# Lanes of 512 and 256 columns in place of twice 384 in the first products of two expert layers

## The chip, the cores and the metric

The program runs on one core of a Trainium2 chip. The metric is the device time of one execution in microseconds, as the median of three runs. PE is the matrix engine (TensorE), DVE is VectorE, ACT is ScalarE, POOL is GpSimd, SP issues DMA transfers.

## The reference, cut to what matters

```
y[t] = scale * q[t] @ state,  state = gamma * state + outer(k[t], v[t])   # 2 batches, 8 heads, 768 steps, head size 64
x = y as 1536 tokens x 512
h = x @ w_in              # 512 -> 2048
x = silu(h) @ w_out       # 2048 -> 512
h = x @ w_in2
out = leaky_relu(h, 0.01) @ w_out2
```

A retention layer feeds two layers that each widen 1536 tokens from 512 to 2048 features, apply a function and narrow again. All is float32; a float32 product is made of three matmuls of rounded parts (high x high, high x low, low x high: `TERMS`).

## The kernel before, in words

The tokens are cut into 12 chunks of 128 and kept transposed: features on the partitions, tokens along the row. For the widening products they form two lanes of N = 768 / 2 = 384 columns on two halves: four column groups s = 0 to 3 of 384 tokens, lane p = s // 2, half s % 2. `xa` holds the even groups, `xb` and `b12` the odd ones, `tm` and `xf` (in the two `big` tiles) the unrounded sums, and `T4[p]` the rounded sums.

The widening takes 16 feature blocks in eight steps of two blocks a layer. A step is a two by two matrix product in seven products (Winograd's form): weights and tokens are added and subtracted first, then seven products make the four results. A product (`product`, L410 on) is six matmuls a lane, and `go` issues lane 0 and then lane 1: 12 matmuls. The order of a step is written out in `rest` (L1018 on): 6, 2, 5, 7, 1 of the next step, 4, 3. Products 1, 6, 7 and 4 accumulate in one PSUM pair X, so ScalarE copies X (`copy`) after 1, 6 and 7 before PE may add to it; VectorE adds results from the banks Z and V to the copies (`add`); ScalarE applies the function (`act`), and `keep` stores the step's result in HBM. The first two steps of layer 0 are `plain`: four results of 24 matmuls each, 12 a lane. The first two steps of layer 1 are issued by `lanes` (L991 on), lane by lane and interleaved, steps a and b, so that lane 0 can begin before lane 1's tokens are there; c is step 2.

The narrowing in layer 0 (`down`, L517 on) has 24 units: three sets of 512 tokens times eight feature blocks, 24 matmuls of 512 columns each. It fetches results with `fetch_g` and rounds them with `split_g`. After the last block of a set `finish_x` copies the sums out. The narrowing of layer 1 is class `Two`: one set of 512 tokens plain and four of 256 in seven products.

Weights come as packed words and are decoded: `words` (ScalarE, two calls; the second writes the tile `u`), `clamp`, `sign` or `signed`, `low` (VectorE). `split_a` and `split_s` round weights and their sums, `keep_s` makes four sums in `u` on VectorE and stores them, `keep_w` stores the words, `fetch_w` brings words back. The order on each engine is the order in which the program issues: tasks in lists (`up_tasks`, `lane_tasks`, `todo`) are called ahead of the product, or unit, with their number. Every engine works off its queue in order.

Of the kernel before, what the change touches and what calls it, by code (L numbers as in the profile page):

```python
# [18 lines left out]
C = 128  # L19
# [9 lines left out]
N = 384  # L29
ORDER = [b * NC + c for c in range(NC) for b in range(B)]  # L30
PER = N // C
# [13 lines left out]
def retention_moe_kernel(ctx: ExitStack, tc: tile.TileContext, att, w1, w2, cst, out):  # L45
# [55 lines left out]
    raw = [sb.tile([128, n, 2, 2, 512], F32, tag=t, name=f"att_{t}") for t, n in (("t1", 3), ("w5", 1), ("t0", 2))]  # L101
# [9 lines left out]
    def two(i, p):  # L111
        return big[i].rearrange("p (a h k n) -> p a h k n", a=2, h=2, k=2)[:, :, p]
# [223 lines left out]
    def place(p):  # L336
        t = free.pop(0)
        b12[p] = [t[:, n, :, 0:N] for n in range(2)]
        return t
# [37 lines left out]

    def store_x(j):
        s, c = divmod(j, PER)
        a, b = c * C, c * C + C  # L380
# [9 lines left out]
    def round_x(j, which=(0, 1)):  # L390
        s, c = divmod(j, PER)
        a, b = c * C, c * C + C
# [34 lines left out]
    class Step:  # L427
        def __init__(self, layer, i):
            self.layer, self.i, self.w = layer, i, (layer, 0, i)
            self.X = None  # L430
            if layer == 0 and i == 0:
                self.g = call.rearrange("p a b n -> p (a b n)").rearrange("p (f s n) -> p f s n", f=2, s=4)
            else:
                b = (i + layer) % 2
                self.g = big[b].rearrange("p (f s n) -> p f s n", f=2, s=4)

        def go(self, n):
# [7 lines left out]
            for p, o in enumerate(getattr(self, t)[0]):  # L445
                product(n, self.w, p, o[:, 0:N], n in (1, 2, 5), n in (2, 3, 4))


        def lane(self, n, p):
# [8 lines left out]
            product(n, self.w, p, o[:, 0:N], n in (1, 2, 5), n in (2, 3, 4))  # L458
# [11 lines left out]

        def block(self, f, half, c=slice(0, 2)):
            return self.g[:, f, half::2][:, c]

        def copy(self, n, x=None):
            for c, t in (x or self.X)[1]:
                nc.scalar.activation(out=ct[n][:, c, 0:N], in_=t[:, :, 0:N], func=AF.Copy)  # L476

        def add(self, f, half, n, t):
            for c, t in t[1]:
                nc.vector.tensor_tensor(  # L480
                    out=self.block(f, half, c), in0=t[:, :, 0:N], in1=ct[n][:, c, 0:N], op=ALU.add
                )

        def act(self, f, half, t=None):
            for c, i in [(slice(0, 2), None)] if t is None else t:
                o = self.block(f, half, c)
                i = o if i is None else i[:, :, 0:N]
# [5 lines left out]
        def keep(self):  # L493
            t = gscr[self.layer, self.i] = dram.tile([128, 2, 4 * N], F32, name=f"g{self.layer}_{self.i}")
            nc.sync.dma_start(out=t.rearrange("p f (s n) -> p f s n", s=4), in_=self.g)
# [8 lines left out]
    def fetch_g(layer, s, i):  # L504
# [4 lines left out]
        nc.sync.dma_start(out=t, in_=gscr[layer, i][:, :, s * T:s * T + T])  # L509
# [19 lines left out]
    def finish_x(s, ya, yb, whole=None):  # L529
        later = []  # L530
        at = s * T
        segments = []
        while at < s * T + T:
            e = min(s * T + T, (at // N + 1) * N)
            segments.append((at - s * T, e - s * T, at // N, at % N))
            at = e
# [14 lines left out]
    class Two:  # L551
# [12 lines left out]
        def load(n, t):  # L564
            s, i = divmod(n, Q)
            m = 256 if s else T
            at = 256 * s + 256 if s else 0
# [51 lines left out]
        def run(self):  # L619
            wt = [three(p) for p in range(2)]  # L620
            x = [sb.tile([128, 3, 4, 256], FR, tag=f"xa{p}", name=f"s{p}") for p in range(2)]
            x = [t[:, n] for t in x for n in range(3)]
            x += [sb.tile([128, 4, 256], FR, tag=f"xb{p}", name=f"s{2 + p}") for p in range(2)]
# [64 lines left out]
            def third(i):  # L688
                return split_2((1, 1, i), wt[(i - 2) // 3][:, (i - 2) % 3])
# [521 lines left out]
```

## Time and profile before

| what | us |
|---|---|
| median of three runs | 546.33 (546.29 to 546.64) |
| the profiled execution | 546.1 |
| its span, first to last instruction | 544.3 |
| TensorE busy | 537.7 |
| VectorE busy | 423.0 |
| ScalarE busy | 308.7 |

The stages as the timeline shows them: retention until 45.8 us, the two plain steps until about 81, the other steps of layer 0 until 167.5, its narrowing until 298.1, the steps of layer 1 until 415.4 and its narrowing until the end. A matmul's length in a row overlaps the next one's, so its price is read from the distance of two starts.

### The profile page before, as it was taken

To read this page: it belongs to the slowest core of one execution; us is meant where nothing else is said; L and a number is where in the kernel's file an instruction comes from. 1 tells how busy PE (TensorE), PEld (TensorE's weight loads), DVE (VectorE), ACT (ScalarE), POOL (GpSimd) and SP (SyncE) were. 2 spreads that over 40 slices of the span, in tenths; PEclk is the share of its full clock that TensorE was granted. 3 is DMA by queue.
4 is the path that set the end of the run, shared out by engine and by line. 5 is a ranking of instruction groups with operands and counts; after the bars stand their busy time and mean duration, and the time that the engine had idled before them with its cause. 6 is when DMAs were issued, how large, how long until landed. Compare 5 with 4: busy or idle time off the path is not lost.

```text
span 544.3 us, 8909 instructions
## 1 busy us (share of the span) xinstructions
PE 537.7 (99%) x3534; PEld 501.0 (92%) x3534; DVE 423.0 (78%) x576; ACT 308.7 (57%) x394; POOL 77.8 (14%) x72
## 2 busy tenths in 40 slices
PE   8999999999999999999999999999999999999996
PEld 6999999999998888888888999999999888999996
DVE  3999979999976885764888876777777478998893
ACT  2257857787766655544445676666556465544341
POOL 2880000344400000001500020322100000000000
PEclk9999999999999999999999999999999999999999
DMA  8992525788789959697284009887648986643521
GB/s 297 417 358 82 178 106 212 275 287 284 221 287 362 359 189 300 197 309 274 80 303 160 2 8 369 323 314 280 243 165 295 384 300 233 198 149 102 157 79 39
DMA packets 41818, 124.92 MB, mean 229 GB/s; under 512 B 3758, under 2 KB 12078, under 8 KB 39728
## 3 DMA queue, kind: packets, MB, share of 16 engines
q1 hardware_dynamic: 41456, 124.01, 64.4%
q8 instruction: 27, 0.44, 0.3%
q10 hardware_dynamic: 288, 0.34, 0.2%
q14 instruction: 15, 0.12, 0.1%
q0 software_dynamic: 32, 0.00, 0.0%
HBM read 83.44 MB, written 40.89 MB: 228 GB/s over the span
## 4 chain that ended last, share of the span: by engine, by line
PE 96%; DVE 2%; DMA 1%; issue 0%; ACT 0%; DVEq 0%; ACTq 0%
PE p L421 22%; PE b L421 16%; PE b L523 12%; PE p L523 12%; PE b L660 8%; PE p L660 6%; PE p L644 4%; PE b L644 4%; PE p L963 3%; PE b L963 3%; PE p L276 2%; PE b L293 2%; PE b L305 1%; DVE c L283 1%; DMA att_t<-att_dram 1%; PE b L319 1%
## 5 line engine op out<-in xcount | busy, mean ns | idle before, releaser
L421 PE MATMUL p<-tt,w 128*128 128x384 f32 x504 | 95.7, 336 | 0.0
L421 PEld LDWEIGHTS p<-tt,w 128*128 128x128 f32 x504 | 88.7, 188 | 0.1
L476 ACT ACTIVATE c<-p 128x768 f32<-128x768 f32 (+1 forms) x48 | 35.1, 731 | 44.9 <-PE p L421 33.7
L480 DVE TENSOR_TENSOR big<-b,c 128x384 f32<-128x384 f32 x84 | 43.6, 550 | 17.8 <-ACT c L476 10.8
L523 PE MATMUL b<-w,wt 128*128 128x512 f32 x216 | 54.8, 389 | 0.0
L523 PE MATMUL p<-w,wt 128*128 128x512 f32 x216 | 54.8, 389 | 0.0
L147 ACT ACTIVATE u<-ws 128x1024 int32<-128x1024 uint32 x32 | 36.4, 1137 | 29.5 <-DVE r L169 28.1
L205 DVE TENSOR_TENSOR w<-c,w 128x1024 fp32r<-128x1024 f32 x23 | 29.9, 1298 | 28.5 <-ACT w L203 28.5
L523 PEld LDWEIGHTS b<-w,wt 128*128 128x128 f32 x216 | 40.6, 188 | 8.4
L523 PEld LDWEIGHTS p<-w,wt 128*128 128x128 f32 x216 | 40.6, 188 | 8.4
L162 DVE SCALAR_TENSOR_TENSOR r<-ws,r 128x1024 int32<-128x1024 int32 x32 | 42.6, 1330 | 0.9
L169 DVE CUSTOM_DVE_ANT_0 r<-r,u 128x2048 uint16<-128x2048 uint16 x32 | 41.3, 1292 | 1.4
L199 POOL TENSOR_TENSOR sf<-r 128x256 f32<-128x256 f32 x18 | 16.8, 955 | 176.1 <-DVE r L169 71.7
L145 ACT ACTIVATE r<-ws 128x1024 f32<-128x1024 f32 x32 | 36.6, 1144 | 8.0 <-DMA ws<-w_dram 6.0
L203 ACT ACTIVATE w<-c 128x1024 fp32r<-128x1024 f32 x23 | 24.4, 1063 | 18.7 <-DMA c<-g 18.7
L421 PE MATMUL b<-tt,w 128*128 128x384 f32 x168 | 32.0, 336 | 0.0
L421 PE MATMUL b<-xb,w 128*128 128x384 f32 x168 | 31.9, 337 | 0.0
L421 PE MATMUL b<-xa,w 128*128 128x384 f32 x168 | 31.9, 337 | 0.0
L421 PE MATMUL p<-xa,w 128*128 128x384 f32 x168 | 31.9, 337 | 0.0
L205 DVE TENSOR_TENSOR w<-sf,w 128x1024 fp32r<-128x1024 f32 x15 | 18.3, 1223 | 15.2 <-ACT w L203 15.2
L421 PEld LDWEIGHTS b<-tt,w 128*128 128x128 f32 x168 | 29.7, 188 | 0.0
L421 PEld LDWEIGHTS p<-xa,w 128*128 128x128 f32 x168 | 29.5, 188 | 0.1
(168 smaller groups left out, 1080.4 us busy)
## 6 DMA issues: line engine op xcount, KB each, us to landing
ws<-w_dram SPq DMA_DIRECT2D x64, 512.0 KB, 5.4
g<-big SPq DMA_DIRECT2D x15, 1536.0 KB, 6.3
c<-g SPq DMA_DIRECT2D x30, 512.0 KB, 7.2
scr<-r SPq DMA_DIRECT2D x16, 512.0 KB, 5.7
r<-scr SPq DMA_DIRECT2D x16, 512.0 KB, 7.6
att_t<-att_dram SPq DMA_DIRECT2D x15, 512.0 KB, 9.4
c<-g SPq DMA_DIRECT2D x17, 256.0 KB, 3.6
r<-g SPq DMA_DIRECT2D x15, 256.0 KB, 3.5
```

Of the source, the lines that this page charges most:

```text
L145: nc.scalar.activation(out=r.bitcast(F32), in_=t[:, :, :, 1].bitcast(F32), func=AF.Abs)
L147: nc.scalar.activation(out=u, in_=t[:, :, :, 0].bitcast(U32), func=AF.Copy, scale=2.0 ** -29)
L162: nc.vector.scalar_tensor_tensor(out=r, in0=t[:, :, :, 1], scalar=-0x40000000, in1=r, op0=ALU.bitwise_and, op1=ALU.bitwise_or)
L169: nc.vector.tensor_tensor(out=r, in0=r, in1=u, op=ALU.add)
L205: nc.vector.tensor_tensor(out=l, in0=s, in1=h.bitcast(F32), op=ALU.subtract)
L421: nc.tensor.matmul(out=o, lhsT=a[:, ta, k * 128:k * 128 + 128], rhs=rhs(p, tb, k), start=(begin and m == 0), stop=(end and m == 5), skip_g ...
L476: nc.scalar.activation(out=ct[n][:, c, 0:N], in_=t[:, :, 0:N], func=AF.Copy)
L480: nc.vector.tensor_tensor(out=self.block(f, half, c), in0=t[:, :, 0:N], in1=ct[n][:, c, 0:N], op=ALU.add)
L523: nc.tensor.matmul(out=y, lhsT=l, rhs=r, start=(i == 0 and f == 0 and n == 0), stop=(i == Q - 1 and f == 1 and n == 2),)
L644: nc.tensor.matmul(out=y[m], lhsT=g[:, tg, c:c + 128], rhs=w[:, tw, 1 - f], start=(i == 0 and f == 0 and k == 0), stop=(i == Q - 1 and f = ...
L660: nc.tensor.matmul(out=y[at][:, 256 * half:256 * half + 256], lhsT=g[:, tg, b], rhs=w[:, tw, a] if sm is None else S[i][tw][:, sm], start= ...
L963: nc.tensor.matmul(out=y[m][0][p][:, 0:N], lhsT=a[:, ta, (A11, A21)[f] + kk // 2, k * 128:k * 128 + 128], rhs=x, start=(i == 0), stop=(i = ...
```

## The change

The lanes become unequal: lane 0 has 512 columns (tokens 0 to 511 on one half, 512 to 1023 on the other), lane 1 has 256 (1024 to 1279, 1280 to 1535). So lane 0 holds the first two sets of the narrowing and lane 1 the third. All tiles that were 384 wide a lane follow: `xa`, `xb`, `T4`, the weights' place `three` (four and two blocks instead of three and three), the result tiles `big` and their place in HBM, from which `fetch_g` now reads a third set in two pieces of 256 columns. Copies and `act` calls over both lanes run over 768 columns in one piece.

```diff
-N = 384
+LANE = (512, 256)
+AT = (0, 512)
+N = sum(LANE)
-PER = N // C
+START = (0, 512, 1024, 1280)
...
-                product(n, self.w, p, o[:, 0:N], n in (1, 2, 5), n in (2, 3, 4))
+                product(n, self.w, p, o[:, 0:LANE[p]], n in (1, 2, 5), n in (2, 3, 4))
...
+        g = gscr[layer, i].rearrange("p f (h n) -> p f h n", h=2)
+        if s < 2:
+            nc.sync.dma_start(out=t, in_=g[:, :, s, 0:T])
+        else:
+            nc.sync.dma_start(out=t.rearrange("p f (h n) -> p f h n", h=2), in_=g[:, :, :, T:N])
...
-            4: lambda: (load_next(), [round_x(j) for j in LATER[:5]]),
+            4: lambda: (load_next(), [round_x(j) for j in LATER[:4]]),
...
-                     (b, 6, 0), (b, 2, 0), (b, 5, 0), (b, 7, 0), (a, 1, 1), (b, 4, 0), (b, 3, 0),
+                     (b, 6, 0), (b, 5, 0), (b, 7, 0), (b, 2, 0), (b, 4, 0), (a, 1, 1), (b, 3, 0),
...
-                if (n, p) == (7, 1):
-                    s.act(0, 0)
...
                 s.lane(n, p)
+                if (n, p) == (7, 1):
+                    s.act(0, 0)
...
-            todo[21] += [lambda: split_s(n0), lambda: high_t(0, 0)]
-            todo[22] += [lambda: left_t(0, 0), lambda: high_t(0, 1)]
-            todo[23] += [lambda: left_t(0, 1), lambda: split_s(n1)]
+            todo[21] += [lambda: split_s(n0)]
+            todo[22] += [lambda: high_t(0, 0), lambda: left_t(0, 0)]
+            todo[23] += [lambda: split_s(n1), lambda: high_t(0, 1), lambda: left_t(0, 1)]
...
-                if n == 21:
+                if n == 22:
                     T4[0] = tt_tile(0)
...
-            at(15, lambda: left_t(1, 1))
-            for m, t in enumerate(up_tasks(1, 1)):
-                at((15, 17, 20, 22, 24, 26, 28, 28)[m], *t)
+            at(14, lambda: left_t(1, 1))
+            w2nd, n2, n3 = second_w[1][1], first_w[Q + 2], first_w[Q + 3]
+            at(9, lambda: words(w2nd, at=-1))
+            at(11, lambda: clamp(w2nd))
+            at(24, lambda: signed(w2nd))
...
+            at(26, lambda: low(w2nd))
+            at(28, lambda: keep_s(w2nd), lambda: keep_w(w2nd))
```

On PE a step of layer 0 stands as follows before; `p` and `b` are PSUM tiles (pairs and single banks), `xa`, `xb` and `tt` (= `T4`) hold tokens, `w` weights, and the numbers only tell buffers apart.

```order
L421 MATMUL p_916<-xa_64,w_669 128x384 x6
L421 MATMUL p_916<-xa_65,w_669 128x384 x6
L421 MATMUL b_989<-tt_667,w_670 128x384 x6
L421 MATMUL b_990<-tt_668,w_670 128x384 x6
```

And the same products now.

```order
L430 MATMUL p_915<-xa_64,w_668 128x512 x6
L430 MATMUL p_915<-xa_65,w_668 128x256 x6
L430 MATMUL b_988<-tt_666,w_669 128x512 x6
L430 MATMUL b_989<-tt_667,w_669 128x256 x6
```

The order of products and the number of matmuls stay; the first lane of each product is longer and the second shorter.

On DVE the end of `lanes` in layer 1, from the rounding of step 2's weights on, before: L480 is `add`, L205 the low half of a rounding, L151 and L155 `clamp`, L162 `sign`, L169 `low`, L183 the sums of `keep_s`, whose store follows them.

```order
L205 TENSOR_TENSOR w_86<-sf,w_86 128x1024
L480 TENSOR_TENSOR big_69<-b_2679,c 128x384 x2
L151 TENSOR_SCALAR r_75<-r_75 128x1024
L155 TENSOR_SCALAR r_75<-r_75 128x1024
L480 TENSOR_TENSOR big_68<-b_2728,c 128x384
L162 SCALAR_TENSOR_TENSOR r_75<-ws_72,r_75 128x1024
L480 TENSOR_TENSOR big_68<-b_2746,c 128x384
L169 ISA r_75<-r_75,u 128x2048
L183 TENSOR_TENSOR u<-r_75 128x256 x2
L183 TENSOR_TENSOR u<-u,r_75 128x256
L183 TENSOR_TENSOR u<-r_75,u 128x256
L480 TENSOR_TENSOR big_68<-b_2746,c 128x384
```

Now (L496 is `add`, L211 the low half, L168 `sign`, L175 `low`, L189 the sums):

```order
L496 TENSOR_TENSOR big_69<-b_2668,c 128x256 x2
L496 TENSOR_TENSOR big_68<-b_2713,c 128x256
L168 SCALAR_TENSOR_TENSOR r_73<-ws_72,r_73 128x1024
L211 TENSOR_TENSOR w_85<-sf,w_85 128x1024
L496 TENSOR_TENSOR big_68<-b_2729,c 128x256
L175 ISA r_73<-r_73,u 128x2048
L189 TENSOR_TENSOR u<-r_73 128x256 x2
L189 TENSOR_TENSOR u<-u,r_73 128x256
L189 TENSOR_TENSOR u<-r_73,u 128x256
L496 TENSOR_TENSOR big_68<-b_2729,c 128x256
```

`clamp` has moved ahead (it now stands among lane 0's work), and the low half of `split_s` has moved behind `sign`; the sums still follow the addition of (b, 2) in lane 1.

On ACT, the copy of product 7 of lane 1 and the function of the result before it, step a, before (L476 and L492 are `copy`, L491 and L507 `act`, L203 and L209 the high half of a rounding):

```order
L476 ACTIVATE c<-p_2525 128x384
L203 ACTIVATE w_86<-sf 128x1024
L491 ACTIVATE big_69<-big_69 128x2x384
L476 ACTIVATE c<-p_2525 128x384
L476 ACTIVATE c<-p_2572 128x384
```

Now:

```order
L209 ACTIVATE w_84<-r_75 128x768
L492 ACTIVATE c<-p_2512 128x256
L507 ACTIVATE big_69<-big_69 128x768
L492 ACTIVATE c<-p_2559 128x256
```

The copy stands ahead of the function, and the high half of `split_s` has moved behind.

## Rows read from the trace of the kernel before

**Rows 1.** The page: engine's busy time, share, instructions; share of the chain that ended last.

```profile
PE 537.7 (99%) x3534; PEld 501.0 (92%) x3534; DVE 423.0 (78%) x576; ACT 308.7 (57%) x394; POOL 77.8 (14%) x72
...
PE 96%; DVE 2%; DMA 1%; issue 0%; ACT 0%; DVEq 0%; ACTq 0%
```

**Rows 2.** Timeline of PE, a step of layer 0: start, length (us), line, operands, count.

```profile
102.52 2.24 PE L421 MATMUL p<-tt,w 128*128 128x384 f32 x12
104.60 2.25 PE L421 MATMUL p<-xa,w 128*128 128x384 f32 x12
106.69 2.27 PE L421 MATMUL p<-tt,w 128*128 128x384 f32 x12
...
115.09 2.27 PE L421 MATMUL b<-tt,w 128*128 128x384 f32 x12
117.20 2.24 PE L421 MATMUL p<-tt,w 128*128 128x384 f32 x12
```

**Rows 3.** Timeline of PE, first row of the down stage and first row behind it.

```profile
167.49 1.52 PE L523 MATMUL b<-w,w 128*128 128x512 f32 x6
...
298.06 1.21 PE L421 MATMUL p<-xa,w 128*128 128x384 f32 x6
```

**Rows 4.** Timeline of PE, last stage, the same place in units 28 apart.

```profile
464.73 0.87 PE L660 MATMUL p<-wt,w 128*128 128x256 f32 x6
...
534.28 0.86 PE L660 MATMUL p<-wt,gh 128*128 128x256 f32 x6
```

**Rows 5.** Timeline of PE, 512 columns with weights from different places (second operand).

```profile
421.00 1.52 PE L644 MATMUL p<-w,w 128*128 128x512 f32 x6
422.36 1.52 PE L644 MATMUL b<-w,w 128*128 128x512 f32 x6
...
426.45 1.56 PE L644 MATMUL p<-wt,gh 128*128 128x512 f32 x6
427.85 1.56 PE L644 MATMUL b<-wt,gh 128*128 128x512 f32 x6
```

**Rows 6.** Groups by line and form, DVE: count, busy us, mean ns, idle before.

```profile
L480 DVE TENSOR_TENSOR big<-b,c 128x384 f32<-128x384 f32 x84 | 43.6, 550 | 17.8 <-ACT c L476 10.8 <-PE b L421 6.1 <-DMA g<-big 0.7
...
L372 DVE TENSOR_TENSOR tt<-big,tt 128x1536 fp32r<-128x1536 f32 x8 | 13.9, 1753 | 3.3 <-ACT tt L368 3.3
...
L677 DVE TENSOR_TENSOR o<-b,o 128x512 f32<-128x512 f32 x8 | 5.5, 692 | 0.8
...
L677 DVE TENSOR_TENSOR o<-p,o 128x256 f32<-128x256 f32 x4 | 1.7, 418 | 4.4 <-ACT o L676 4.4
```

**Rows 7.** Timelines of DVE and of PE, layer 0: one addition three steps apart, and PE.

```profile
98.98 1.01 DVE L480 TENSOR_TENSOR big<-b,c 128x384 f32<-128x384 f32 x2
...
143.21 1.01 DVE L480 TENSOR_TENSOR big<-b,c 128x384 f32<-128x384 f32 x2
...
144.45 2.27 PE L421 MATMUL b<-tt,w 128*128 128x384 f32 x12
```

**Rows 8.** Timeline of ACT, first copy of layer 1.

```profile
299.36 0.49 ACT L476 ACTIVATE c<-p 128x384 f32<-128x384 f32 x1 [1.12 <-PE p L421]
```

**Rows 9.** Timelines of PE, DVE, SP and ACT, end of `lanes` and step 2 of layer 1.

```profile
322.14 1.21 PE L421 MATMUL b<-xa,w 128*128 128x384 f32 x6
...
339.94 2.27 PE L421 MATMUL p<-tt,w 128*128 128x384 f32 x12
...
323.39 0.56 DVE L480 TENSOR_TENSOR big<-b,c 128x384 f32<-128x384 f32 x1 [0.20 <-PE b L421]
...
329.36 0.33 SPq L185 DMA_DIRECT2D scrs<-u  x1
...
336.75 1.18 ACT L147 ACTIVATE u<-ws 128x1024 int32<-128x1024 uint32 x1 [1.41 <-DMA scrs<-u]
...
338.56 0.80 ACT L476 ACTIVATE c<-p 128x768 f32<-128x768 f32 x1
```

**Rows 10.** Transfers of `scrs`, the stored sums: from issue to landing.

```profile
DMA to landing us min/median/max: 2.6/3.9/10.0
```

More of the change, by code (lines that the diff above doesn't have):

```diff
@@ L337, in place @@
         t = free.pop(0)
-        b12[p] = [t[:, n, :, 0:N] for n in range(2)]
+        b12[p] = [t[:, n, :, 0:LANE[p]] for n in range(2)]
         return t
@@ L376, in split_t, with columns @@
         left_t(p, n)
+    def columns(j):
+        s = max(n for n in range(4) if START[n] <= j * C)
+        return s, j * C - START[s], j * C - START[s] + C
     def store_x(j):
-        s, c = divmod(j, PER)
-        a, b = c * C, c * C + C
+        s, a, b = columns(j)
         y = yu[j]
@@ L469, in lane, with cols @@
                 self.add(0, 1, 1, t(o))
+        @staticmethod
+        def cols(c, t=None):
+            if t is None:
+                return slice(AT[c.start], AT[c.stop - 1] + LANE[c.stop - 1])
+            return t.rearrange("p a n -> p (a n)")[:, 0:sum(LANE[c])]
         def block(self, f, half, c=slice(0, 2)):
-            return self.g[:, f, half::2][:, c]
+            return self.g[:, f, half, self.cols(c)]
         def copy(self, n, x=None):
             for c, t in (x or self.X)[1]:
-                nc.scalar.activation(out=ct[n][:, c, 0:N], in_=t[:, :, 0:N], func=AF.Copy)
+                nc.scalar.activation(out=flat[n][:, self.cols(c)], in_=self.cols(c, t), func=AF.Copy)
         def add(self, f, half, n, t):
@@ L480, in add @@
                 nc.vector.tensor_tensor(
-                    out=self.block(f, half, c), in0=t[:, :, 0:N], in1=ct[n][:, c, 0:N], op=ALU.add
+                    out=self.block(f, half, c), in0=self.cols(c, t), in1=flat[n][:, self.cols(c)], op=ALU.add
                 )
@@ L493, in keep @@
         def keep(self):
-            t = gscr[self.layer, self.i] = dram.tile([128, 2, 4 * N], F32, name=f"g{self.layer}_{self.i}")
-            nc.sync.dma_start(out=t.rearrange("p f (s n) -> p f s n", s=4), in_=self.g)
+            t = gscr[self.layer, self.i] = dram.tile([128, 2, 2 * N], F32, name=f"g{self.layer}_{self.i}")
+            nc.sync.dma_start(out=t.rearrange("p f (h n) -> p f h n", h=2), in_=self.g)
         def done(self):
@@ L530, in finish_x @@
         later = []
[L531 to L536, printed above, removed]
+        segments = [(START[n] - s * T, START[n] - s * T + LANE[n // 2], n, 0) for n in range(4) if START[n] // T == s]
         for k, y in ((1, yb), (0, ya)):
@@ L566, in load @@
             m = 256 if s else T
-            at = 256 * s + 256 if s else 0
+            at = (0, N, N + 256, T, N + T)[s]
             nc.sync.dma_start(
@@ L620, in run @@
             wt = [three(p) for p in range(2)]
-            x = [sb.tile([128, 3, 4, 256], FR, tag=f"xa{p}", name=f"s{p}") for p in range(2)]
-            x = [t[:, n] for t in x for n in range(3)]
-            x += [sb.tile([128, 4, 256], FR, tag=f"xb{p}", name=f"s{2 + p}") for p in range(2)]
+            x = [sb.tile([128, n, 4, 256], FR, tag=t, name=f"s{t}") for t, n in (("xa0", 4), ("xa1", 2), ("xb0", 2))]
+            x = [t[:, n] for t in x for n in range(t.shape[1])]
             S = [x[2 * n:2 * n + 2] for n in range(4)]
@@ L818, in retention_moe_kernel @@
             0: load_next, 2: lambda: (words(wa), clamp(wa)), 3: lambda: (signed(wa), low_a()),
-            4: lambda: (load_next(), [round_x(j) for j in LATER[:5]]),
-            5: lambda: ([round_x(j) for j in LATER[5:]], words(wb), clamp(wb), signed(wb)),
+            4: lambda: (load_next(), [round_x(j) for j in LATER[:4]]),
+            5: lambda: ([round_x(j) for j in LATER[4:]], words(wb), clamp(wb), signed(wb)),
         }
```

39 lines of the change are left out of this document (22 added, 17 removed).

## The prediction

> **What bounds the kernel now.** I read the page first: TensorE is busy for 537.7 of the 544.3 us and the chain that ended last is 96% PE [rows 1]. Then TensorE's timeline: from 45.8 us on no row shows idle time, so each product starts when the one ahead lets it. Two things can therefore move the end: the distance from one matmul's start to the next, and a wait that does not exist today.
>
> The distances come from starts, since a matmul's own length overlaps the next one. A step is seven products of 12 matmuls. From 102.52 to 117.20 us the 84 matmuls of 384 columns take 14.68 us, 174.8 ns each [rows 2]. The same rows show that the price depends on what came before: a product that reads `tt` after one that also read `tt` takes 2.08 us (173.3 ns a matmul), `xa` or `xb` after `tt` 2.09, and `tt` after `xa` or `xb` 2.11. Seven times 2.08 would be 14.56, so these changes of operand cost 0.12 us a step. The down stage has 576 matmuls of 512 columns from 167.49 to 298.06 us: 226.7 ns each [rows 3]. The last stage has 588 matmuls of 256 columns between 464.73 and 534.28 us (28 units of 21): 118.3 ns each [rows 4].
>
> **The shapes.** Number of matmuls and sum of columns stay; each pair 384 + 384 becomes 512 + 256. A step becomes 42 x 226.7 + 42 x 118.3 = 9.52 + 4.97 = 14.49 us, 0.19 less. There are six such steps in layer 0 and eight in layer 1 (two of them in `lanes`, by lane, in the same number): 14 x 0.19 = 2.7 us. The two `plain` steps have 96 matmuls of 384 each, 16.78 us at 174.8 ns, and will have 48 x 345.0 ns = 16.56: 0.22 each, 0.4 together. That is 3.1 us, the upper bound of the gain. It supposes that the changes of operand go, as the rows of the down stage show none. But that stage doesn't alternate between operands and the new steps still do. The lower bound from the same rows: 173.3 ns at 384 and 226.7 at 512 lie on a line of 0.417 ns a column plus 13.3 ns; on it 256 columns cost 120.0, a step 42 x 346.7 ns = 14.56, and with the 0.12 kept it is 14.68 again: gain nought. I take the measured 118.3, which also comes from a stage that alternates, and half of the changes: 3.1 - 14 x 0.06 - 0.1 = **2.2 us** gained.
>
> One row goes further down. In the last stage's first unit 512 columns take 1.36 us per six when weights come from `w`, but 1.40 when they come from a `gh` that lies in the place of `ws` [rows 5]: 233.3 ns instead of 226.7. There it is the stationary operand; in lane 0 `xa` and `xb` are the moving one, and at 384 columns they cost no more than `tt`. I leave it out of the sum and keep it as the third rival.
>
> **Vector and scalar work.** Copies and `act` calls over both lanes keep their 768 elements. An addition of 384 took 550 ns, twice 1.10; 512 and 256 take 692 and 418, together 1.11 [rows 6]. The copies of `finish_x` become fewer. All of it lies beside PE. What counts is where PE arrives sooner than its partners.
>
> First, layer 0. VectorE's additions for one product of successive steps start at 98.98 and 143.21 us, three steps apart: 14.74 us a step, PE 14.68 [rows 7]. At 143.21 lane 0's addition ends 0.55 us later, and PE writes that bank at 144.45: 0.69 us left. The addition of 512 ends 0.14 later, and with a PE step of about 14.55 four steps lose another 4 x 0.13 = 0.52. So 0.03 remain: **0**; with the full shape gain (4 x 0.19) it would be a wait of some 0.2, bounds 0 to 0.3.
>
> Second, lane 1 in `lanes`. A product of a lane shrinks from 1.04 to 0.71 us. Between the end of (a,7) and the start of (a,4) lies one product, and the copy of 7 must be through. Such a copy began at 299.36, 0.26 us after its product was issued in full (298.06 + 6 x 0.173), and takes 0.49 at 384 elements and 0.80 at 768, so 0.39 at 256 [rows 3, 8, 9]: 0.65 of 0.71. The change puts this copy ahead of `act(0, 0)`, which keeps it so. Price 0 to 0.1, taken 0.05.
>
> Third, step 2 of layer 1. Its product 4 waits for the copy of product 7, which stands on ScalarE behind the second half of `words`; that half writes `u` and waits until the store of `u` issued by `keep_s` has landed. Before: product (b,2) of lane 1 starts at 322.14 and product 4 at 339.94, 17.80 later. The addition behind (b,2) starts at 323.39, the store is issued 5.97 later, `u` is free 7.3 after that (336.75 less the start-up), and the copy ends at 339.36, 0.58 before PE needs it [rows 9]. After: 3 x 0.71 + 2.07 + 2 x 0.71 + 5 x 2.07 = 15.97 us from (b,2) to product 4. The addition starts at 0.71 + 0.21 = 0.92. Behind it VectorE has, start to start, the addition itself (0.34), `sign` (1.14), the low half of `split_s` (1.14), an addition (0.34), `low` (1.25) and the four sums (1.55): 5.8. With the same 7.3 for the store and 2.7 to the end of the copy that is 16.7: PE waits **0.7 us**. The moved `clamp` and `words` stand earlier and hide behind lane 0. The bounds lie in the store: the transfers of this kind landed between 2.6 and 10.0 us after issue [rows 10], this one with the 1.5 MB store of `g` just ahead of it on the same queue. A landing within 6.6 us removes the wait, one of 10 makes it 3.4. I take 7.3, the row at this very place.
>
> `T4[0]` is now made after unit 21 instead of 20, so its first half is rounded in unit 22. Unit 21 ends at 167.49 + 22 x 5.44 = 287.2 (24 units in 130.57 us), and (a,5) reads the half 12 us later. VectorE's share of a rounding takes 1.75 us at 1536 elements [rows 6], some 2.3 at 2048, ScalarE's comes ahead of it; the splits of `n0` and `n1` and the four sums that stand between fill the rest only in part. Cost nought; if that cover went, (a,5) waits for what is left over.
>
> **Sum.** 546.1 (the profiled execution, 544.3 of span and 1.8 around it) - 2.2 + 0.7 + 0.05 + 0 = 544.65. The median of the three runs is 0.23 above this execution, so 544.9 on the median.
>
> **Rivals.** (1) Full shape gain and the store lands sooner: -3.1 with 0.2 to 0.9 of waits, 543.4 to 544.1. For it: six matmuls of 512 columns from like places take the same 1.36 us in each row [rows 5]. Against: every us PE gains makes the waits above longer. (2) No gain in the shapes: cost is linear in columns and the changes of operand stay, so 0 to -0.5 with 0.7 of waits: 546.3 to 547. For it: the line through 384 and 512. The Trainium skill, in "TensorE: Matmul & The Clock Gate", section "Back-to-back issue gap", gives a warm gap of N / 2.4 plus a fixed 2.5 ns; by it both splits of 768 columns cost 325 ns and the shapes bring nothing. The trace has 13.3 where the page has 2.5, but agrees that 384 and 512 lie on a line; 118.3 at 256 lies below it. (3) Slower: 512 columns with operands from unlike places cost 233.3 [rows 5]. If all 684 matmuls of lane 0 do, that is +4.5 against -3.1, with 0.8 of waits +2.2: 548.5. It decides from 231.2 ns (349.5 - 118.3) on, where a pair costs the old 349.5. If only the 324 that read `xa` or `xb` do, it is +2.1, and the end stays within 0.2 of today.
>
> **How the numbers follow.** Forecast 0.40, own range 544.1 to 545.7; rival 1 0.17; rival 2 (with the milder form of 3) 0.29; rival 3 0.14. A measurement of this kernel can tell about 0.2%, 1.1 us, from no change: faster means below 545.2, slower above 547.4. Faster: 0.17 and 0.24 of the forecast = 0.41. Within: 0.16 of the forecast and 0.26 of rival 2 = 0.42. Slower: 0.14 and 0.03 = 0.17. Range 543.9 to 547.7: it leaves out the best of rival 1 and the worst of rival 3.
>
> **What would show it.** In the trace after: a step of layer 0 in 14.5 to 14.6 us (shapes right), 14.68 or more (rival 2 or 3), with six lane-0 matmuls at 1.36 against 1.40 telling rival 3; a PE gap of some 0.7 us before product 4 of step 2 of layer 1, released by the copy, with `u` waiting for the store just ahead on ScalarE; no gap at the change of layers above 0.1. The prediction is wrong if PE idles anywhere else, or if the pair 512 + 256 costs more than 349.5 ns.

## The result

The changed kernel takes 551.42 us (549.69 to 551.63, six runs) where the kernel before takes 546.22: a ratio of 1.009, interval 1.0077 to 1.0103. The forecast was 544.9 with a range of 543.9 to 547.7, so it was wrong in sign and size. The profiled execution of after took 551.4 us against 546.1, and its span 549.4 against 544.3. Its mean granted clock of 0.996 holds a fall that is shown below; two more of the six executions have 0.996 (spans of 549.1 and 549.6 us), and three have 0.999 (547.6 to 548.8), which leaves no room for such a fall.

The page says first that TensorE's busy time grew by only 2.5 us and that the chain that ended last, 96% PE before [rows 1], now runs through VectorE and ScalarE too. From the page of after, engines and chain:

```profile
PE 540.2 (98%) x3534; PEld 472.8 (86%) x3534; DVE 427.7 (78%) x573; ACT 307.9 (56%) x385; POOL 82.0 (15%) x72
...
PE 86%; DVE 7%; ACT 3%; DMA 2%; issue 2%; DVEq 0%; ACTq 0%; SPq 0%
```

TensorE's timeline of after, one row for the start of each stage (start us, length, engine, line, operands, count). Starts are what is read; where the window that was asked for ends inside a row, here and further down, its length and count cover only the part inside:

```profile
45.64 4.70 PE L977 MATMUL p<-xa,w 128*128 128x512 f32 x19
...
167.51 1.53 PE L543 MATMUL b<-w,w 128*128 128x512 f32 x6
...
298.08 1.56 PE L430 MATMUL p<-xa,w 128*128 128x512 f32 x6
...
420.47 1.56 PE L658 MATMUL p<-w,gh 128*128 128x512 f32 x6
```

| stage | before, us | after, us |
|---|---|---|
| steps of layer 0 (45.8 to 167.5) | 121.65 | 121.87 |
| narrowing of layer 0 | 130.57 | 130.57 |
| steps of layer 1 | 117.36 | 122.39 |
| narrowing of layer 1, to the end of the span | 128.9 | 128.9 |

Two things can be seen in it. Layer 0, which held some 1.1 us of the gain forecast, gained nothing: the shapes bring nothing there. And the whole loss of 5.03 us lies in the steps of layer 1.

A step of layer 0 after the change, which answers to [rows 2]:

```profile
102.48 2.26 PE L430 MATMUL p<-tt,w 128*128 128x512 f32 x12
104.58 2.28 PE L430 MATMUL p<-xa,w 128*128 128x512 f32 x12
106.69 2.24 PE L430 MATMUL p<-tt,w 128*128 128x512 f32 x12
108.77 2.28 PE L430 MATMUL b<-xb,w 128*128 128x512 f32 x12
...
117.16 1.09 PE L430 MATMUL p<-tt,w 128*128 128x512 f32 x4
```

The step is 117.16 - 102.48 = 14.68 us, to the hundredth what it was. The order of prices has turned round, though: before, `tt` behind `xa` was the dear one (2.11) and `xa` cost 2.09; now `xa` and `xb` cost 2.11 to 2.12, `tt` behind them 2.08, and `tt` behind `tt` 2.10 instead of 2.08.

The change of layers, timeline of PE (in brackets the idle time ahead and what ended it):

```profile
299.48 0.40 PE L430 MATMUL b<-tt,w 128*128 128x512 f32 x1
301.53 1.43 PE L430 MATMUL b<-tt,w 128*128 128x512 f32 x5 [1.65 <-DVE tt L378]
303.31 2.93 PE L430 MATMUL p<-tt,w 128*128 128x512 f32 x6 [0.35 <-ACT c L492]
306.03 1.73 PE L430 MATMUL b<-xa,w 128*128 128x512 f32 x6
```

and the stretch behind them by engine and granted clock (us, busy us and count for PE, PEld, DVE, ACT and POOL, PEclk, DMA share, GB/s):

```profile
303.31:306.44 3.13, 3.13 (x8) 2.51 (x8) 1.50 (x1) 1.15 (x4) 0.00 (x0) 0.51 0.00 0
```

The second product waits, one matmul in, for the low half of `T4[0]` (`left_t(0, 0)`, L378): 2.05 us from start to start instead of 0.23, and the next start comes 0.11 late. The third waits for the copy of the first (L492): another 0.52. Behind these two waits the granted clock is 0.51, the lower level of 1.2 GHz, over 3.13 us: seven matmuls, which take some 1.61 at full clock, lose 1.5. Before, the same stretch had a clock of 1.00 and no idle time.

At step 2 of layer 1, timelines of PE, ACT, SP, DVE and POOL:

```profile
342.03 2.27 PE L430 MATMUL p<-xa,w 128*128 128x512 f32 x12
344.85 1.43 PE L430 MATMUL p<-tt,w 128*128 128x512 f32 x5 [0.54 <-ACT c L492]
...
342.20 1.16 ACT L153 ACTIVATE u<-ws 128x1024 int32<-128x1024 uint32 x1 [1.60 <-DMA scrs<-u]
...
336.65 0.33 SPq L191 DMA_DIRECT2D scrs<-u  x1
...
328.93 0.42 DVE L496 TENSOR_TENSOR big<-b,c 128x256 f32<-128x256 f32 x1 [1.06 <-PE b L430]
331.87 1.65 DVE L175 CUSTOM_DVE_ANT_0 r<-r,u 128x2048 uint16<-128x2048 uint16 x1
333.55 1.73 DVE L189 TENSOR_TENSOR u<-r 128x256 f32<-128x256 f32 x2
...
331.70 2.42 POOL L205 TENSOR_TENSOR sf<-r 128x256 f32<-128x256 f32 x2 [58.31 <-DVE w L211]
```

This is the wait that the prediction named, in its place: product 4 starts 0.70 us after the one ahead of it would let it (342.03 + 2.12 = 344.15), with 0.1 more on the next matmul.

The account of the profiled execution: 1.82 + 0.11 + 0.52 of waits at the change, 1.5 of clock, 0.80 at step 2, 0.07 in lane 1: 4.8 of the 5.03 us. What is left, 0.2, is spread over dearer products, in the lanes and in the steps behind them.

### The profile page after: what moved, and what is told of

Its sections match the earlier page's. It is cut to its first block, busy times and chain, and to the rows that moved or that the text cites. A ratio compares the mean times of both kernels' runs of the same rounds, so it can differ in the third digit from the quotient of the medians.

```text
span 549.4 us, 8898 instructions
## 1 busy us (share of the span) xinstructions
PE 540.2 (98%) x3534; PEld 472.8 (86%) x3534; DVE 427.7 (78%) x573; ACT 307.9 (56%) x385; POOL 82.0 (15%) x72
## 4 chain that ended last, share of the span: by engine, by line
PE 86%; DVE 7%; ACT 3%; DMA 2%; issue 2%; DVEq 0%; ACTq 0%; SPq 0%
PE p L430 20%; PE b L430 15%; PE b L674 8%; PE b L543 8%; PE p L543 8%; PE p L674 6%; PE p L658 4%; PE b L658 4%; PE p L977 3%; PE b L977 3%; PE p L282 2%; DVE w L211 2%; PE b L299 2%; PE b L311 2%; PE b L325 1%
## 5 line engine op out<-in xcount | busy, mean ns | idle before, releaser
L430 PE MATMUL p<-tt,w 128*128 128x512 f32 (+1 forms) x504 | 97.1, 340 | 0.9 <-ACT c L492 0.9
L430 PEld LDWEIGHTS p<-tt,w 128*128 128x128 f32 x504 | 81.0, 191 | 12.3 <-ACT c L492 1.8
L492 ACT ACTIVATE c<-p 128x768 f32<-128x768 f32 (+2 forms) x48 | 35.0, 732 | 46.3 <-PE p L430 32.9
L496 DVE TENSOR_TENSOR big<-b,c 128x512 f32<-128x512 f32 (+1 forms) x84 | 43.5, 551 | 20.7 <-ACT c L492 10.4
L211 DVE TENSOR_TENSOR w<-c,w 128x1024 fp32r<-128x1024 f32 x23 | 29.5, 1282 | 28.2 <-ACT w L209 28.2
L168 DVE SCALAR_TENSOR_TENSOR r<-ws,r 128x1024 int32<-128x1024 int32 x32 | 44.4, 1387 | 0.9
L205 POOL TENSOR_TENSOR sf<-r 128x256 f32<-128x256 f32 x18 | 17.5, 991 | 175.7 <-DVE r L175 71.4
L175 DVE CUSTOM_DVE_ANT_0 r<-r,u 128x2048 uint16<-128x2048 uint16 x32 | 41.9, 1309 | 1.8 <-DVE r L168 0.5
L151 ACT ACTIVATE r<-ws 128x1024 f32<-128x1024 f32 x32 | 36.6, 1144 | 8.9 <-DMA ws<-w_dram 6.6
L209 ACT ACTIVATE w<-c 128x1024 fp32r<-128x1024 f32 x23 | 24.2, 1060 | 19.3 <-DMA c<-g 19.2
L430 PE MATMUL b<-tt,w 128*128 128x512 f32 (+1 forms) x168 | 32.0, 337 | 1.6 <-DVE tt L378 1.6
L430 PE MATMUL b<-xa,w 128*128 128x512 f32 (+1 forms) x168 | 32.4, 340 | 0.0
L430 PE MATMUL b<-xb,w 128*128 128x512 f32 (+1 forms) x168 | 32.2, 339 | 0.0
L430 PE MATMUL p<-xa,w 128*128 128x512 f32 (+1 forms) x168 | 32.2, 339 | 0.0
L430 PEld LDWEIGHTS b<-tt,w 128*128 128x128 f32 x168 | 26.7, 189 | 5.4 <-DVE tt L378 2.1
L430 PEld LDWEIGHTS b<-xa,w 128*128 128x128 f32 x168 | 27.2, 190 | 3.8
```

Source lines behind the costliest of these rows:

```text
L151: nc.scalar.activation(out=r.bitcast(F32), in_=t[:, :, :, 1].bitcast(F32), func=AF.Abs)
L168: nc.vector.scalar_tensor_tensor(out=r, in0=t[:, :, :, 1], scalar=-0x40000000, in1=r, op0=ALU.bitwise_and, op1=ALU.bitwise_or)
L175: nc.vector.tensor_tensor(out=r, in0=r, in1=u, op=ALU.add)
L211: nc.vector.tensor_tensor(out=l, in0=s, in1=h.bitcast(F32), op=ALU.subtract)
L430: nc.tensor.matmul(out=o, lhsT=a[:, ta, k * 128:k * 128 + 128], rhs=rhs(p, tb, k), start=(begin and m == 0), stop=(end and m == 5), skip_g ...
L492: nc.scalar.activation(out=flat[n][:, self.cols(c)], in_=self.cols(c, t), func=AF.Copy)
```

## Experiments

Theory after the result: (P) the operands' places, that is, where their tiles start in a partition of the on-chip memory, and the hand-over between column counts set what a product costs, so the shapes bring nothing; (G) the four operations on lane 0's sums that GpSimd does in unit 18 grew from 768 to 1024 elements, and VectorE, slowed beside them, delivers everything behind them late. Rivals: the waits come from the order in which `T4` and the splits are issued, from the redone order as a whole, or from the 512 columns themselves. Every kernel was timed against the kernel before on its chip.

### Shapes: places of the operands

e1_after_place and e2_before_place move three small tiles, which shifts the start of `xa` and `xb`, and of the tiles behind them (`ws`, and so `gh`, among them), from 224 bytes behind a multiple of 512 to the multiple itself, where `tt` and the weights lie. Below, two operands in like places both start at the multiple or both 224 bytes behind one; otherwise their places are unlike.

```diff
+    z = sb.tile([128, 256], BF, name="z")
+    z1 = sb.tile([128, 1], F32, name="z1")
+    one = sb.tile([1, 64], F32, name="one")
     xa = [sb.tile([128, 2, NP, LANE[p]], FR, tag=f"xa{p}", name=f"xa{p}") for p in range(2)]
```

> The changed kernel, with the three small tiles z, z1 and one made ahead of xa, so that xa, xb, big, c and ws begin at a multiple of 512 bytes in their partition, as the weights and tt do (before: 224 behind one). Nothing else moves. Theory P (the operand's place costs): six matmuls of 512 columns from xa or xb take 1.36 us instead of 1.39, a product 2.08, a step of layer 0 14.55 us instead of 14.68; 14 such steps give 1.8 us, and the last stage 0.8, since its 120 matmuls with a gh from a ws place fall from 233.3 to 226.7 ns. In all -2.8, 548.6 us. Theory H (the hand-over from 256 to 512 columns costs, whatever the place): tt after tt, both at multiples of 512, costs 2.100 in the changed kernel, so every product would, a step 14.70, and only the last stage gains: 550.6 us.

> The kernel before (lanes of 384 and 384), with the same move of z, z1 and one. Theory P: every product takes the 2.08 us that tt after tt takes, a step 14.56 instead of 14.68; 14 steps give 1.7 us, the last stage 0.8: 543.6 us. Theory C (a change of operand costs, not its place): steps stay at 14.68, only the last stage gains 0.8: 545.4 us.

Measured: e1 551.57 us (ratio 1.0095, 1.0079 to 1.0111), e2 545.05 (0.9977, 0.9968 to 0.9985). The steps in PE's timeline, first e1, then e2:

```profile
102.56 2.26 PE L430 MATMUL p<-tt,w 128*128 128x512 f32 x12
104.67 2.26 PE L430 MATMUL p<-xa,w 128*128 128x512 f32 x12
...
117.27 1.09 PE L430 MATMUL p<-tt,w 128*128 128x512 f32 x4
```

```profile
102.20 2.24 PE L421 MATMUL p<-tt,w 128*128 128x384 f32 x12
104.28 2.24 PE L421 MATMUL p<-xa,w 128*128 128x384 f32 x12
...
116.76 1.55 PE L421 MATMUL p<-tt,w 128*128 128x384 f32 x8
...
144.29 2.00 PE L421 MATMUL b<-tt,w 128*128 128x384 f32 x10
```

With like places every product costs the same, whatever stands ahead of it: 2.10 us at 512 and 256 columns (14.71 a step), 2.08 at 384 and 384 (14.56). So P holds for the kernel before and H for the changed one: unlike places cost 0.12 us a step at 384, and at 512 + 256 the hand-over costs as much again once the places are like. The kernel before, so placed, is the faster one, although 0.9 us of the gain goes into new waits at the end of layer 0, so that the 543.6 us of theory P are missed. The row at 144.29 starts 2.29 us after the one ahead (142.00) instead of 2.08: VectorE, whose additions came every 14.74 us in [rows 7], does not follow a step of 14.56.

The last stage went the other way than both theories said. PE's timeline of e2 at the place of [rows 4]:

```profile
463.36 0.88 PE L660 MATMUL p<-wt,w 128*128 128x256 f32 x6
...
533.92 0.88 PE L660 MATMUL p<-wt,gh 128*128 128x256 f32 x6
```

588 matmuls in 70.56 us are 120.0 ns each, where [rows 4] give 118.3. So the 118.3 was not the price of 256 columns, but of 256 columns with many operands in unlike places. With like places 256, 384 and 512 columns cost 120.0, 173.3 and, by the down stage, 226.7 ns: one line, N / 2.4 + 13.3.

e8_before_xa shifts `xa` and `xb` (with `big` and `c`, which lie between them and `ws`) to the multiple, and leaves `ws` (and so `gh`) where it was.

```diff
+    z1 = sb.tile([128, 1], F32, name="z1")
+    one = sb.tile([1, 64], F32, name="one")
     xa = [sb.tile(...) for p in range(2)]
...
+    pad0 = sb.tile([128, 56], F32, name="pad0")
     ws = [sb.tile([128, 2, 512, 2], I32, tag=f"ws{i}", name=f"ws{i}") for i in range(2)]
```

> The kernel before, with xa and xb at a multiple of 512 bytes as tt and the weights, but ws still 224 behind one (two small pads), so that only the places of the steps and of s change, not the place of gh in the last stage. Place theory: a step with no wait 14.56 us, as in e2_before_place; the last stage 123.97 us or up to 0.3 less, where e2_before_place had 124.35, since 256 columns from unlike places take 117.5 to 118 ns and from like places 119 to 120; the 0.8 us of new waits at 135 to 151 us stay, since VectorE needs 14.7 us a step there: 544.5 us. Rival: the last stage was longer in e2_before_place for another reason, and stays at 124.35: 545.0 us.

Measured 544.75 us (0.9974, 0.9963 to 0.9984), the fastest kernel of this study. Outside the waits, products take 2.08 us. From the start of the last stage to the end of its last matmul it is 123.6 us, 0.4 less than before, where at most 0.3 was expected. PE's timeline of e8 in that stage:

```profile
459.80 1.21 PE L663 MATMUL b<-s,gh 128*128 128x256 f32 x9
460.85 0.51 PE L663 MATMUL b<-w,gh 128*128 128x256 f32 x3
```

These nine matmuls take 1.05 us, 116.7 ns each. In the kernel before the same nine, from 460.79 to 461.87, took 120.0: there `s` (in the place of `xa`) and `gh` both lay 224 bytes behind a multiple, and here only `gh` does. So it is the two places against each other that count, and the place theory holds in this stage as well. Waits of 0.3 us remain, at 150 us.

e11_before_256 puts the tiles that e2 moves 256 bytes behind a multiple (a pad of 32 bytes ahead of `xa`).

> The kernel before, with xa, xb, big, c, ws, r, u and sf moved by 32 bytes, so that they begin 256 bytes behind a multiple of 512 instead of 224; weights and tt stay at a multiple of 512. If like places mean equal remainders of 512 bytes: products with xa and xb still 2.09 and tt behind them 2.11 us, 546.2 us. If a remainder of 256 counts as like (or only multiples of 64 matter): products 2.08 us, and as e8_before_xa or e2_before_place: 544.6 to 545.1 us.

Measured 545.36 us (0.9982, 0.9973 to 0.9991), 0.3 above what was expected; products 2.08 us, and in the last stage 120.0 ns at 256 columns. So a start 256 bytes behind counts as like, and what matters is not the remainder of 512 bytes. Which remainders beside 224 are dear was not tried: those of 64 and of 256 bytes would both fit. In the profiles it differs from e8 by 0.8 us in the last stage and by 1.0 in the waits at the end of layer 0.

### The change of layers: order or GpSimd

e3_after_t4 and e6_after_late change the order alone.

```diff
-            todo[22] += [lambda: high_t(0, 0), lambda: left_t(0, 0)]
-            todo[23] += [lambda: split_s(n1), lambda: high_t(0, 1), lambda: left_t(0, 1)]
+            todo[22] = [lambda: high_t(0, 0), lambda: left_t(0, 0), lambda: high_t(0, 1)] + todo[22]
+            todo[23] += [lambda: split_s(n1), lambda: left_t(0, 1)]
```

e6 has `left_t(0, 1)` in unit 22 too, and `split_s(n1)` ahead of the fifth product of the lanes.

> The changed kernel, with the rounding of T4[0] put first in unit 22 (high 0, left 0, high 1 ahead of low and the splits of n1) instead of last in units 22 and 23. Theory Q (left_t(0, 0) stands last on VectorE and the second high_t stands ahead of a copy on ScalarE): the idle times of 1.8 and 0.5 us at the change of layers go, and with them the 1.55 us that seven matmuls lose at the clock of 0.50 behind them: about -4.0, 547.4 us. Rival W (the weights' chain is late by 2.7 us, whatever order T4 has): something of n1 or of a copy is late instead, 1 us or more of idle time stays within 8 us of the change, and the clock falls again: 549.5 to 551.4 us.

> The changed kernel, with both halves of T4[0] ahead of low and the splits of n1 in unit 22, and split_s(n1) moved from unit 23 to the fifth product of the lanes. Nothing is done about GpSimd. Theory Q2 (ScalarE's half of split_s(n1) waits for VectorE's four sums and holds back the copy behind it): the 2.5 us of idle time at the sixth to twelfth matmul pair go, and the half clock with it; about -4.0 against the changed kernel, 547.4 us, at most 0.5 us of new idle time at the additions of lane 0. Rival W (VectorE is late whatever the order): an idle time above 1 us at another product of the first ten, and the half clock behind it: 550 us or more.

Measured: e3 552.39 us (1.0117, 1.0103 to 1.0132), e6 549.18 (1.0055, 1.0042 to 1.0068). PE and ACT of e3, then of e6:

```profile
303.97 1.93 PE L430 MATMUL p<-tt,w 128*128 128x512 f32 x6 [2.34 <-ACT c L492]
...
301.83 1.06 ACT L209 ACTIVATE w<-sf 128x1024 fp32r<-128x1024 f32 x1 [2.55 <-DVE sf L205]
```

```profile
302.73 1.66 PE L430 MATMUL p<-tt,w 128*128 128x512 f32 x6 [1.19 <-ACT c L492]
...
300.80 0.85 ACT L209 ACTIVATE w<-r 128x768 fp32r<-128x768 f32 x1 [5.99 <-DVE r L175]
```

In both the wait for `tt` is gone, and another has come: the copy of the first product stands on ScalarE behind a rounding of n1 that waits for VectorE. Theories Q and Q2 fell, and in both the wait of rival W is there: VectorE is late whatever the order. With e3 the clock fell again (0.50 behind an idle time of 2.34 us); with e6 it stayed at 1.00 behind 1.19, and the 550 us of rival W were not reached, while e3 came out 1.0 above what rival W gave. So the order is not the cause of the lateness, but it has a say in how much of it reaches TensorE: e6 is 2.2 us faster than the changed kernel.

e5_after_dve takes GpSimd out and leaves the order, the new place of `T4[0]` included, as the change made it.

```diff
-                        todo[n + 3] += [lambda: first_t(0, nc.gpsimd), lambda: rest_t(0, nc.gpsimd)]
+                        todo[n + 3] += [lambda: first_t(0, nc.vector), lambda: rest_t(0, nc.vector)]
```

> The changed kernel, with the four operations of first_t and rest_t of lane 0 in unit 18 on VectorE instead of GpSimd; all else in place. Theory G (GpSimd's four operations of 1024 elements slow VectorE beside them, and this makes the weights' chain late): VectorE's four slowed operations fall from 11.5 to 3.8 us in all and four of 1.2 us come, so VectorE is some 2.8 us further at 274, the words of n1 land as early as in the kernel before, the 1.8 and 0.5 us of idle time at the change go and with them the 1.55 us at half clock: 547.4 to 548 us. Rival T (the order of T4 and of the splits alone does it): VectorE's own four operations cost what the contention cost, or the idle time stays above 1.5 us: 551 us.

Measured 547.71 us (1.0024, 1.0014 to 1.0034): theory G, 3.7 us better than the changed kernel. VectorE and, beside it, GpSimd in after, with `left_t(0, 0)` ahead of GpSimd's rows; then VectorE in e5:

```profile
265.45 2.89 DVE L157 TENSOR_SCALAR r<-r 128x1024 f32<-128x1024 f32 x1
268.38 2.77 DVE L161 TENSOR_SCALAR r<-r 128x1024 int32<-128x1024 int32 x1
271.18 3.30 DVE L168 SCALAR_TENSOR_TENSOR r<-ws,r 128x1024 int32<-128x1024 int32 x1
...
299.19 2.28 DVE L378 TENSOR_TENSOR tt<-big,tt 128x2048 fp32r<-128x2048 f32 x1
...
264.54 3.25 POOL L365 TENSOR_TENSOR big<-big 128x1024 f32<-128x1024 f32 x1 [5.79 <-DVE xb L211]
267.87 2.72 POOL L369 TENSOR_TENSOR big<-big,big 128x1024 f32<-128x1024 f32 x1
270.55 2.84 POOL L370 TENSOR_TENSOR big<-big,big 128x1024 f32<-128x1024 f32 x1
```

```profile
264.76 0.69 DVE L157 TENSOR_SCALAR r<-r 128x1024 f32<-128x1024 f32 x1
...
295.42 2.29 DVE L378 TENSOR_TENSOR tt<-big,tt 128x2048 fp32r<-128x2048 f32 x1
```

VectorE's operations end 0.55 to 1.1 us behind GpSimd's, one for one: at 268.34 behind 267.79, at 271.15 behind 270.59, at 274.48 behind 273.39. Beside GpSimd an operation of 0.69 us takes as long as GpSimd's does. The Trainium skill has this in "SBUF — State Buffer", section "SBUF: two separate sides": VectorE and GpSimd share a pair of ports, and for VectorE operations that need this pair (those with two inputs from the on-chip memory, or in a mode that uses both ports) it is an exclusive lock held for the whole instruction, so the other waits. These rows agree with it; which mode VectorE's one-input operations ran in, no row tells. In e5 `left_t(0, 0)` begins at 295.42 instead of 299.19, and TensorE does not wait at the change.

In the kernel before the same thing was there, in smaller size (timelines of VectorE and GpSimd):

```profile
268.47 2.22 DVE L155 TENSOR_SCALAR r<-r 128x1024 int32<-128x1024 int32 x1
...
296.43 3.42 DVE L372 TENSOR_TENSOR tt<-big,tt 128x1536 fp32r<-128x1536 f32 x2
...
267.85 2.29 POOL L364 TENSOR_TENSOR big<-big,big 128x768 f32<-128x768 f32 x1
```

It was covered there: the first of the two `left_t` in the last row ended at 298.18, and the second product began at 299.10 with its second matmul, the first to read that half, 0.17 later. The slack was 1.1 us. GpSimd's three operations now end at 273.39 instead of 270.14. VectorE's next `sign`, which frees the weights' place, starts at 281.57 instead of 279.65, the load behind it lands 3.8 us after its issue instead of 3.0, and the words of n1 are 2.7 us late. `left_t(0, 0)` starts 2.8 us later and, with 2048 elements, takes 0.5 longer; the slack and a first product that is 0.4 longer take up 1.5 of this, and TensorE waits for the rest.

e10_before_pool and e12_before_pool8 bring the cause into the kernel before: three and eight more subtractions of 256 elements on GpSimd in unit 18, on a tile of their own.

```diff
+                        todo[n + 3] += [lambda: nc.gpsimd.tensor_tensor(out=extra, in0=extra, in1=extra, op=ALU.subtract)] * 3
```

> The kernel before, with three more subtractions of 256 elements on GpSimd behind rest_t of lane 0 in unit 18, on a small tile that nothing else reads. They make GpSimd busy for some 2 to 3 us more there, about what lanes of 512 columns added. Theory G (GpSimd's time beside VectorE makes the weights' chain late, whatever the lanes): VectorE is 1 to 2 us later at 282, left_t(0, 0) ends at 299 to 300.2 where TensorE needs it at 299.1, and TensorE waits 0 to 1.1 us there: 546.2 to 547.5 us, and VectorE's operations from 270 to 276 us are slowed by a factor of 2 or more beside the three. Rival (the lateness comes from the 512 columns themselves): VectorE at 282 stays within 0.3 us of before, no wait, 546.2 us.

> As e10_before_pool, with eight extra subtractions instead of three, so GpSimd is busy some 9.7 us more in unit 18 (1.21 us each). In e10_before_pool three of them put VectorE 1.1 us back against TensorE, and TensorE just began to wait (0.10 us at 299.89). Theory G: eight put VectorE some 2.4 to 3.0 us back at 282, about as far as the changed kernel's lanes did; TensorE waits 1.3 to 2.2 us for left_t(0, 0) one product behind the down stage, 0 to 0.6 us for the copy of the first product, and the clock may fall behind it as it does in the changed kernel: 547.8 to 550.5 us. Rival (lanes of 512 columns themselves cause the waits): a wait of at most 0.3 us, 546.5 us.

Measured: e10 546.29 us (1.0002, 0.9994 to 1.0011), e12 547.56 (1.0024, 1.0015 to 1.0032). VectorE starts its next `sign`, counted from the start of the narrowing, 1.1 and 2.2 us later than in the kernel before. PE, POOL and DVE of e12:

```profile
300.13 1.14 PE L423 MATMUL b<-tt,w 128*128 128x384 f32 x5 [1.01 <-DVE tt L374]
...
269.75 8.99 POOL L1148 TENSOR_TENSOR extra<-extra 128x256 f32<-128x256 f32 x8
...
276.05 1.47 DVE L185 TENSOR_TENSOR sf<-r 128x256 f32<-128x256 f32 x2
```

In e10 the slack is just used up (TensorE waits 0.09 and 0.10 us at the two matmuls behind the first); in e12 it waits 1.18 and 0.11 us, at the very matmul of after, with lanes of 384 columns. So neither 512 columns nor the new order is needed for the wait, and the rival falls. In time e10 came out at the lower end of what theory G gave and e12 0.2 us below it: these small operations of GpSimd slow VectorE by a factor of 1.2 to 2, not 2 and more.

e4_before_order keeps lanes of 384 and takes of the change only the redone order of `lanes` and of the tasks behind it; `T4[0]` stays where it was.

> The kernel before with lanes of 384 and 384, and of the change only the order of work at the change of layers (the order of products in the lanes, act(0, 0) behind the copy, and the new places of words, clamp, sign, splits, sums and keep_s); T4[0] stays at unit 21. Theory S (the shapes and what they do to VectorE and GpSimd cause the loss, the order doesn't): no idle time of TensorE above 0.1 us, 546.2 us, within 0.3. Rival O (the new order itself makes the waits): idle time at the change of layers or at step 2 of layer 1, 547.5 us or more.

Measured 547.23 us (1.0018, 1.001 to 1.0027): theory S missed, by 0.7 us, and O's 547.5 was not reached either. PE and ACT:

```profile
314.42 1.33 PE L421 MATMUL p<-tt,w 128*128 128x384 f32 x6 [0.24 <-ACT c L476]
...
312.50 1.49 ACT L368 ACTIVATE tt<-big 128x1536 fp32r<-128x1536 f32 x1
313.88 0.48 ACT L476 ACTIVATE c<-p 128x384 f32<-128x384 f32 x1
```

A copy stands behind `high_t(1, 1)`. With products of 1.04 us that is too late by 0.4, and smaller waits stand at 307 and 311: 0.9 in all, the loss of this kernel. In the changed kernel, where a product of lane 0 that takes 1.4 us stands ahead, the same copy is late by only 0.07 (the second matmul of the row at 322.16), which is the wait of lane 1 in the account. So the new order fits the new lanes, and it carries 0.07 of their loss.

### Step 2 of layer 1, and what is left

e7_after_words issues the second half of `words`, which writes `u`, two products later in step 2.

```diff
-            at(2, lambda: words(w, at=-1))
+            at(2, lambda: words(w, (0,) if k == 2 else (0, 1), -1))
+            if k == 2:
+                at(4, lambda: words(w, (1,)))
```

> The changed kernel, with the second half of words (the write of u) in step 2 of layer 1 issued two products later, behind copy(2). Theory U (the write of u waits for the store of u, and copy(2) stands behind it): the idle time of 0.62 us at 344.03 goes and nothing takes its place, -0.7: 550.7 us, with the change of layers as before. Rival: the copy or VectorE is late for another reason (sign, low and the sums), idle time of 0.4 us or more stays within two products: 551.4 us.

Measured 549.50 us (1.0058, 1.0045 to 1.0071). PE and ACT:

```profile
343.19 2.24 PE L430 MATMUL p<-tt,w 128*128 128x512 f32 x12
...
341.90 0.79 ACT L492 ACTIVATE c<-p 128x768 f32<-128x768 f32 x1
342.59 1.13 ACT L153 ACTIVATE u<-ws 128x1024 int32<-128x1024 uint32 x1
```

The copy now precedes the write of `u`, and TensorE goes through, product 4 starting at 343.19 with no idle time in its row: theory U, as to the wait. The time fell by more than the 0.8 us of that wait, to 1.2 below what U gave. In the profile of this kernel the clock stayed at 1.00 behind the waits at the change (1.56 and 0.35 us idle), where in the profile of after it had fallen and cost 1.5; this part of the gain is not the edit's, as far as the rows show.

e9_after_both has the edits of e5 and e7 together.

> The changed kernel with the edits of e5_after_dve and e7_after_words together: first_t and rest_t of lane 0 on VectorE, and the write of u in step 2 of layer 1 behind copy(2). It asks what the shapes alone are worth once the waits are gone. Theory Z (the shapes bring nothing: a step takes 14.68 us in both kernels): 547.7 - 0.7 = 547.0 us, which is the kernel before plus the 0.4 us of VectorE's waits at the end of layer 0 and about 0.3 of the lanes; TensorE idle nowhere above 0.2 us from 152 us on. Rival (shapes gain and were hidden by waits): 545.2 us or less.

Measured 547.30 us (1.0016, 1.0008 to 1.0025). TensorE waits nowhere in the steps for more than 0.1 us any more, and the kernel is 1.15 us slower than before, not faster: theory Z. In its profile 0.4 of that is a later start of the steps (46.21; in the profiles of this study it lies between 45.5 and 46.4, so this part need not be the shapes'), 0.2 the steps of layer 0, 0.25 those of layer 1 and 0.3 the last stage; the 0.4 us of waits in layer 0 that were expected did not come.

## Why the prediction was wrong, and where it was right

Two steps failed: the price of the shapes, which should have gained 2.2 us and lost about 0.4, and the cover of `T4[0]`, which was priced at nought and cost 4.0. With both put right the sum of 544.9 comes to 551.5, where 551.42 was measured.

**The shapes: -2.2 forecast, +0.2 measured in layer 0 and about as much in layer 1.** The step that failed is the term 42 x 226.7 + 42 x 118.3. Both prices were taken from stages that run one column count for long. The 118.3 was 1.7 ns below the 120.0 of like places (e2) because many operands of that stage lay in unlike ones; it was no price of 256 columns as such. The 226.7 holds for `tt` behind `xa` alone: from `xa` the products cost 2.11, which is the 233 ns of [rows 5] in the moving operand. The prediction had this row and set it aside because `xa` and `tt` cost much the same at 384; the milder form of its rival 3, where only the matmuls that read `xa` or `xb` pay it, had this part right. And the "half of the changes" that should go did not: with like places, where 384 + 384 has no change-over cost at all, 512 + 256 pays 0.02 a product (e1). Rival 2's reason, the line through 384 and 512, was right: with like places 256 columns lie on it too. The Trainium skill, in "TensorE: Matmul & The Clock Gate", section "Back-to-back issue gap", has the same slope in its formula for an isolated matmul; the traces agree with the slope and have 13.3 ns where the page has 2.5.

**`T4[0]` and the change of layers: 0 forecast, 4.0 measured in the profiled execution** (2.45 of waits and 1.5 of clock). The prediction had named a gap at the change of layers above 0.1 us as a sign against it. The sentence "(a,5) reads the half 12 us later" counted TensorE's time from the end of unit 21. VectorE's queue decides: `left_t` stands there behind the decoding, the rounding and the sums of n1, and its slack was 1.1 us, which the trace of before shows. The prediction counted VectorE's own longer rounding (0.5 us) and left out GpSimd's longer operations, whose rows stood in that trace beside the slowed ones. No rival had this mechanism. The clock's part came behind the waits in the profile, and was in no term.

**Step 2: 0.7 forecast, 0.70 and 0.1 measured**, with the named mechanism (e7). Its two inner terms were both off, and cancelled, so that the size was hit by luck. From the addition to the store it took 7.7 us, not 5.8: `low` and the sums took 1.65 and 3.1 us beside the sums that GpSimd does there. The store landed in 5.5, not 7.3. TensorE's own way from (b,2) to product 4 was 0.2 longer than forecast, since the shapes gained nothing.

**Lane 1: 0.05 forecast, 0.07 measured**, but elsewhere: ahead of (a,6), behind the copy of product 1. Ahead of (a,4), where the prediction looked, it was 0.03. **VectorE in layer 0:** no wait was forecast without a shape gain, and none came; the kind of wait that was forecast for a full gain, 0.3 at most, is there wherever a step of 384 columns takes 14.56 us (e2 0.9 us, e11 1.3, e8 0.3), and is mostly longer.

The range missed because it allowed only losses that the prediction had named: its slow end was the price of 512 columns, and the cover of `T4[0]`, on which 4 us hung, had a price of nought and no upper bound.

## What to carry to other kernels

Before pricing a shape by another stage's matmuls, compare the places of both operands and what stands ahead of each: in this kernel the same 256 columns cost 117 or 120 ns, and the same 512 cost 227 or 233. When a change makes one engine's operations longer, look in the trace for what the neighbour does beside them, and follow the neighbour's queue to the next thing that TensorE needs; the slack to bound is the one at the end of that queue, not the time since a tile came free. In this kernel two moved lines and two pads (e8, 0.26% faster) were worth more than the new shapes.

## What the runs showed of the hardware

- Operands 224 bytes behind a multiple of 512, against operands at the multiple, cost 512 columns 6.6 ns a matmul (233.3 against 226.7) and 384 columns 1.4 on average over a step, and gave 256 columns back 3.3 (116.7 against 120.0); with both operands 224 bytes behind, or one 256 bytes behind, 256 columns cost 120.0 again (before, e1, e2, e8, e11).
- A product of six 512 and six 256 columns with like places takes 2.10 us, while two times six of 384 take 2.08.
- VectorE beside GpSimd's operations of 1024 elements needs 2.8 us for what takes 0.69 alone, and ends 0.55 us behind the operation beside it (after, e5).
- The granted clock fell to 0.51 for about 3.1 us behind waits in after, and to 0.50 in e1 and e3, where TensorE had been idle for 1.65, 1.83 and 2.34 us at a stretch; it stayed at 1.00 in e7, e6 and e12, where it had been idle for 1.56, 1.19 and 1.01. What decides it is not shown.
